# Gathering the tails of q, k and v once, starting loads by the state of the queue, and converting weights one piece ahead

## The chip, the cores and the metric

The kernel runs on one core of one Trainium2 chip. The metric is device time in microseconds (us) of one execution. An execution has five engines at work side by side: TensorE (PE, with its weight loads shown apart as PEld), VectorE (DVE), ScalarE (ACT), GpSimd (POOL) and SyncE (SP). Here SP issues nearly all DMA transfers, one after the other, and 16 DMA engines carry them out. Each engine works through its own instructions in the order in which the program was written; an instruction that waits for another engine or for a transfer holds up everything behind it on its engine.

## The reference

```
def sm_attn(qq, kk, vv):                       # 8 batches, 8 heads, sequence 576, head size 64
    s = scale * qq @ kk.T
    a = exp(s - max(s)); a = a / (sum(a) + 1e-9)
    return a @ vv
p_packed = sm_attn(p, k, v)                    # 32 packed rows a head
x = sm_attn(q, p_packed, p_packed)             # as [8, 576, 512], the 8 heads side by side
u = x + (x.T @ U @ V).T                        # U: 576x32, V: 32x576, mixing along the sequence
out = u + relu(u @ w1) @ w2                    # w1: 512x2048, w2: 2048x512
```

q, k, v and p are float32; U, V, w1 and w2 are float64 and come to the chip as pairs of 32-bit words, so that the kernel itself turns them into float32.

## The kernel before, in words

**Main work.** The last line of the reference is nearly all of the arithmetic. It runs in two sweeps over the eight batches, each with one half of the 2048 inner columns, in 8 slices of 128. For each slice `gemm1` makes relu(u w1) for 128 columns (12 matmuls 128x288 into h_ps; the packed attention is folded into the weights beforehand, so that w1 appears as wth and wtl), ACT and DVE split the result into a high part hh and a low part hl, and `gemm2` of the slice before adds 12 matmuls 128x512 into o. Each product is three matmuls (high by high, high by low, low by high; lines 166 to 170).

**Side work.** Everything else that the first sweep needs is written as chains, Python generators that yield after each step: `turn_p` (line 416) and `packs` (430) make the packed rows of a batch, once for each group g of four heads, from k and v; `load_q` (493), `attention` (500) and `mixing` (527) make u of a batch, and store it as its parts ah and al; `fold` (582) makes wth and wtl of a batch and a quarter of the columns; `convert` (273) turns pieces of w1 and w2 into float32, and `uv_chain` (319) does so for U and V.

**Who sets the order.** The class `Chains` (lines 19 to 102) is a planner that runs while the program is written. It keeps a clock of its own, times at which it thinks that ACT, DVE, POOL and the DMA queue (`free`) and the PSUM banks come free, and counts of shared buffers (`xt`, the tiles into which q, k and v are loaded; `ppT`, `wt` and so on). After each piece of gemm1 and gemm2 the kernel calls `place`, which emits up to four steps of chains that are ready by this model, the one with the earliest due time first; `until` (97) emits steps until the chains named are done, with no gemm between. The times are guesses in the source, such as `step(0, ("DMA", 4.3))` for the loads of k and v of one group; `HOP` is the guess for the way from one engine to the next. What comes out is a fixed order of instructions on each engine. At run time nothing of the planner is left: an engine meets its instructions in that order, and waits where data isn't there.

**Loads.** A tile `xt` holds 576 rows of 4 heads: the first 512 rows (the main part, 512 KB) by one DMA (`load_main`, 355), the other 64 (the tail) by four DMAs of 16 KB for k and q (`load_x`, 361) or two of 32 KB for v (`load_v`, 368). Loads of k and v of one batch and group thus are eight DMAs, those of q of a batch ten.

**Conversion.** A piece is 512 KB of float64. `load_bits` brings it into one of two buffers `bits`, by one or two DMAs. `float32_1` (223) takes the absolute value of the high words on ACT into the one tile `ts` (line 227), then works on it with two DVE operations (228, 229) into `wd`; `float32_2` (231) adds sign and low bits with two more (233, 234), and then the buffer is free and the load of the piece after next is issued. For w2 an ACT copy makes the high part w2h (301) and POOL the low part (302). A first chain converts 16 pieces in batch 0 (numbered from 0 below; pieces 0 to 3 are the first quarter of w1, 4 and 5 the first two of w2), the later ones the other halves of w2 and w1.

**The start.** Before the first gemm the kernel emits `until("attention0", "fold000", "w2_0")` (645). Batch b+1 starts its gemms when its `attention` and `fold` chains are done.

## Time and profile before

| what | value |
| --- | --- |
| median of 3 runs | 929.35 us (926.53 to 931.5) |
| profiled execution, its own time | 931.87 us |
| its span, first to last instruction | 930.0 us |
| mean granted TensorE clock | 0.934 of full speed |
| PE busy | 839.7 us, 90% of the span |
| DVE, ACT, POOL busy | 432.5, 313.2, 93.9 us |
| DMA | 73,369 packets, 105.48 MB, 113 GB/s |
| read from and written to DRAM | 70.84 MB and 33.63 MB |
| DMAs for tails in groups of four heads | 64 for k, 64 for q (16 KB each), 32 for v (32 KB each) |

A row of a timeline gives the start, the duration, the engine, the line of the kernel, the operation, the tile written and the tile read, and in brackets how long the engine had been idle and who ended that. A row of the stretches gives the stretch, its length, the busy time of each engine with the number of its instructions, the granted TensorE clock as a part of full speed (PEclk), the busy share of the DMA engines and the rate. "SPq" is the time in which SP issues a DMA.

### The profile page before, as it was taken

Reading aid. Unit: us, or ns where it says so; the run is one execution under the profiler, and the core shown is the slowest. Engines: PE = TensorE matmul, PEld = TensorE weight load, DVE = VectorE, ACT = ScalarE, POOL = GpSimd, SP = SyncE. Lnnn points to the kernel's source line nnn. Section 1 sums busy time; section 2 is a strip of 40 time slices with the busy share of each in tenths; the row PEclk is TensorE's granted clock in tenths of the full one; section 3 lists DMA queues with packets and bytes.
Section 4 is the critical chain, followed back from the end, with each engine's and each line's share of the span. In section 5 each row is a group of like instructions: output and inputs, shape, how many; then the busy total and the mean of one; then the engine's idle time right before and its main releaser. Section 6 shows DMA issues by size and latency. Waiting matters only on the chain.

```text
span 930.0 us, 15444 instructions
## 1 busy us (share of the span) xinstructions
PE 839.7 (90%) x5760; PEld 668.7 (72%) x5760; DVE 432.5 (47%) x1154; ACT 313.2 (34%) x949; POOL 93.9 (10%) x111
## 2 busy tenths in 40 slices
PE   4467488999997899999979999999999999999997
PEld 2336256766875586886667887888888888888886
DVE  1774576364576455543735742342324232432332
ACT  2542244433444434443332422232223222222220
POOL 0121123011122112110111200000000000000000
PEclk9757569998997999999979999999999999999999
DMA  8627642243368443431212242721224040404022
GB/s 209 182 75 216 163 135 83 95 124 121 118 208 256 123 118 135 130 109 48 74 77 77 97 142 74 261 71 72 68 97 143 1 152 13 142 28 137 21 71 68
DMA packets 73369, 105.48 MB, mean 113 GB/s; under 512 B 15952, under 2 KB 47056, under 8 KB 73296
## 3 DMA queue, kind: packets, MB, share of 16 engines
q1 hardware_dynamic: 72976, 103.45, 35.0%
q10 hardware_dynamic: 320, 1.05, 0.5%
q8 instruction: 46, 0.75, 0.3%
q14 instruction: 27, 0.22, 0.1%
HBM read 70.84 MB, written 33.63 MB: 112 GB/s over the span
## 4 chain that ended last, share of the span: by engine, by line
PE 80%; DMA 7%; DVE 6%; ACT 3%; issue 2%; SPq 1%; POOL 0%; ACTq 0%; DVEq 0%
PE o L168 16%; PE o L169 15%; PE o L170 15%; PE h_ps L168 7%; PE h_ps L169 7%; PE h_ps L170 7%; PE t_ps L589 4%; PE t_ps L382 3%; DMA bits<-in_moe_w_ch_dram 2%; PE t_ps L399 2%; PE t_ps L409 2%; PE t_ps L543 1%; DMA sum<-ev 1%; PE t_ps L474 1%; DMA xt<-in_v_dram 1%
## 5 line engine op out<-in xcount | busy, mean ns | idle before, releaser
L691 DVE SCALAR_TENSOR_TENSOR hl<-h_ps,hh 128x256 fp32r<-128x256 f32 x256 | 108.1, 422 | 278.1 <-ACT hjh L689 277.5
L168 PE MATMUL o<-w2h,hh 128*128 128x512 f32 x512 | 212.9, 416 | 3.3 <-DVE ev L715 2.5
L689 ACT ACTIVATE hh<-h_ps 128x256 fp32r<-128x256 f32 x256 | 98.4, 386 | 335.5 <-PE h_ps L170 335.4
L169 PE MATMUL o<-w2l,hh 128*128 128x512 f32 x512 | 203.2, 397 | 1.4 <-POOL w2l L302 1.4
L170 PE MATMUL o<-w2h,hl 128*128 128x512 f32 x512 | 202.8, 396 | 0.0
L168 PE MATMUL h_ps<-ah,wth 128*128 128x288 f32 x512 | 160.1, 313 | 2.4 <-ACT ah L562 1.9
L169 PE MATMUL h_ps<-al,wth 128*128 128x288 f32 x512 | 155.8, 304 | 0.3
L170 PE MATMUL h_ps<-ah,wtl 128*128 128x288 f32 x512 | 155.2, 303 | 0.0
L168 PEld LDWEIGHTS o<-w2h,hh 128*128 128x128 f32 x512 | 97.5, 191 | 42.0 <-issue 21.2
L168 PEld LDWEIGHTS h_ps<-ah,wth 128*128 128x128 f32 x512 | 100.4, 196 | 19.1 <-issue 12.3
L170 PEld LDWEIGHTS o<-w2h,hl 128*128 128x128 f32 x512 | 97.5, 190 | 21.4
L169 PEld LDWEIGHTS o<-w2l,hh 128*128 128x128 f32 x512 | 97.7, 191 | 14.9 <-POOL w2l L302 2.2
L169 PEld LDWEIGHTS h_ps<-al,wth 128*128 128x128 f32 x512 | 100.2, 196 | 5.0 <-POOL al L563 1.4
L170 PEld LDWEIGHTS h_ps<-ah,wtl 128*128 128x128 f32 x512 | 100.4, 196 | 0.0
L593 DVE TENSOR_TENSOR wtl<-t_ps,wth 128x512 fp32r<-128x512 f32 x64 | 41.2, 686 | 49.8 <-ACT wth L592 49.7
L592 ACT CAST wth<-t_ps 128x512 fp32r<-128x512 f32 x64 | 34.4, 589 | 51.6 <-PE t_ps L589 51.6
L383 ACT COPY xT<-t_ps 128x512 f32<-128x512 f32 x64 | 37.1, 588 | 41.4 <-PE t_ps L382 41.2
L382 PE MATMUL t_ps<-ident,xt 128*128 128x128 f32 x256 | 44.0, 307 | 7.5 <-DMA xt<-in_k_dram 4.6
L689 ACT ACTIVATE hjh<-h_ps 128x32 fp32r<-128x32 f32 x256 | 50.0, 195 | 0.0
L382 PEld LDWEIGHTS t_ps<-ident,xt 128*128 128x128 f32 x256 | 34.7, 158 | 16.2 <-DMA xt<-in_k_dram 4.7
L691 DVE SCALAR_TENSOR_TENSOR hjl<-h_ps,hjh 128x32 fp32r<-128x32 f32 x256 | 46.2, 181 | 0.0
L589 PE MATMUL t_ps<-w1t,ppT 64*32 64x512 f32 x512 | 39.1, 644 | 3.6 <-DVE xT L389 1.5
(120 smaller groups left out, 954.1 us busy)
## 6 DMA issues: line engine op xcount, KB each, us to landing
xt<-in_k_dram SPq DMA_DIRECT2D x16, 512.0 KB, 4.8
xt<-in_v_dram SPq DMA_DIRECT2D x16, 512.0 KB, 4.6
xt<-in_q_dram SPq DMA_DIRECT2D x16, 512.0 KB, 4.5
bits<-in_moe_w_ch_dram SPq DMA_DIRECT2D x16, 512.0 KB, 3.8
sum<-ev SPq DMA_DIRECT2D x32, 256.0 KB, 2.3
part<-sum SPq DMA_DIRECT2D x32, 256.0 KB, 6.2
out_dram<-ev SPq DMA_DIRECT2D x32, 256.0 KB, 2.5
bits<-in_moe_w_ch_dram SPq DMA_DIRECT2D x28, 256.0 KB, 4.7
```

The lines of the kernel that those rows point to most:

```text
L168: nc.tensor.matmul(ps, lhsT=lh, rhs=rh, start=start, stop=False)
L169: nc.tensor.matmul(ps, lhsT=lh, rhs=rl, start=False, stop=False)
L170: nc.tensor.matmul(ps, lhsT=ll, rhs=rh, start=False, stop=stop)
L382: nc.tensor.transpose(t_ps[:, P * a:P * a + P], pairs[:, P * c:P * c + P], ident)
L383: nc.scalar.copy(t[:, 2 * h2:2 * h2 + 2, HT:HS], t_ps.rearrange("p (h x) -> p h x", h=2))
L399: nc.tensor.matmul(ss[r][hs, :HS], lhsT=lT[rs, g, hs], rhs=t[rs, h, HT * (1 - r):HT * (1 - r) + HS], start=True, stop=True)
L409: nc.tensor.transpose(t_ps[:, o:o + P], src[:, BLOCK[kk]:BLOCK[kk] + P], ident)
L589: nc.tensor.matmul(f_ps[g][xs], lhsT=ppT[b][gs, g, xs], rhs=w1_slice(x, 2 * sw + c)[gs], start=True, stop=True)
L592: nc.scalar.copy(hi[:, g], f_ps[g])
L593: nc.vector.tensor_tensor(lo[:, g], f_ps[g], hi[:, g].bitcast(F32), op=ALU.subtract)
L689: nc.scalar.activation(hi, src, AF.Relu)
L691: nc.vector.scalar_tensor_tensor(lo, src, 0.0, hi.bitcast(F32), op0=ALU.max, op1=ALU.subtract)
```

## The change

Three things change.

1. A new chain `gather` copies the tails of all of k, q and v from the inputs to three tensors in DRAM, laid out as the `xt` tiles want them: one DMA for k, one for q, eight for v, 3 MB in all. It is due right after q of batch 0 is loaded. The `packs` chains wait for it in the plan. For b > 0 `load_x` and `load_v` then issue two DMAs each, the main part and one tail of 64 KB. Batch 0 loads its tails as before.
2. In the plan a chain with `load=True` (`packs`, and `load_q` for b > 0) starts only when the modelled DMA queue is through. The guessed costs of loads, and of a hop, change, and the `xt` buffers go from 7 to 6.
3. In `convert` the absolute value of piece i+1 is emitted right behind the DVE part of `float32_1` of piece i, with two `ts` tiles, and not at a step of its own; the pause with the due time now lies between `float32_1` and `float32_2`, and a piece of w1 goes on to the next without the planned wait.

All line numbers of the changed kernel are higher than those of before, by 4 at the conversion, by some 30 at the loads and behind.

```diff
--- before.py
+++ after.py
@@ -26,7 +26,8 @@
-    HOP = 0.12
+    HOP = 0.2
 
     def __init__(self, banks, **resources):
         self.now, self.left, self.done, self.flags = 0.0, {}, {}, set()
@@ -35,8 +36,8 @@
         self.resources = resources
         self.slow, self.horizon = 1.0, 0.0
 
-    def add(self, name, due, gen, after=(), need=0, take=()):
-        self.left[name] = dict(due=due, at=self.now, end=self.now, gen=gen, after=after, need=need, take=take)
+    def add(self, name, due, gen, after=(), need=0, take=(), load=False):
+        self.left[name] = dict(due=due, at=self.now, end=self.now, gen=gen, after=after, need=need, take=take, load=load)
 
     def give(self, *names):
         for n in names:
@@ -45,6 +46,7 @@
     def ready(self, name):
         c = self.left[name]
         return (c["at"] <= self.now
+                and (not c["load"] or self.free["DMA"] <= self.now)
                 and (c["due"] <= self.horizon or max(self.free["DVE"], self.free["ACT"]) <= self.now)
                 and all(n in self.flags or n in self.done and self.done[n] <= self.now for n in c["after"])
                 and all(t <= self.now for t in self.banks[:c["need"]])
@@ -65,7 +67,7 @@
         c = self.left[name]
         for r in c["take"]:
             self.resources[r] -= 1
-        used = c["need"]
+        used, c["load"] = c["need"], False
         try:
             pe, ops, c["need"], c["take"], due, wait, c["after"] = next(c["gen"])
             at = self.spend(pe, ops)
@@ -157,7 +159,7 @@
     HM = SM // 2
     HT = ST // 2
     MAIN = (slice(0, HM), slice(HS + HT, S))
-    NX = 7
+    NX = 6
 
     LEAST = 1.125 * 2.0 ** -15
 
@@ -212,7 +214,7 @@
         return pipe.tile([P, 512], I32, name="wd", bufs=2)
 
     def test_tile():
-        return pipe.tile([P, 512], F32, name="ts", bufs=1)
+        return pipe.tile([P, 512], F32, name="ts", bufs=2)
 
     def out_tile(dtype=F32):
         return pipe.tile([P, 512], dtype, name="ev", bufs=3)
@@ -220,11 +222,12 @@
     def bits_tile():
         return pipe.tile([P, 512, 2], I32, name="bits", bufs=2)
 
-    def float32_1(x, t, raw):
-
-
-        high = raw[:, :, 1]
-        nc.scalar.activation(t, high.bitcast(F32), AF.Abs)
+    def float32_0(t, raw):
+        nc.scalar.activation(t, raw[:, :, 1].bitcast(F32), AF.Abs)
+
+    def float32_1(x, t):
+
+
         nc.vector.tensor_single_scalar(t, t, LEAST, op=ALU.max)
         nc.vector.tensor_scalar(x, t.bitcast(I32), 3, 0x3FFFFFF8, op0=ALU.logical_shift_left, op1=ALU.bitwise_and)
 
@@ -234,7 +237,8 @@
         nc.vector.scalar_tensor_tensor(out.bitcast(I32), low, 29, x, op0=ALU.logical_shift_right, op1=ALU.bitwise_or)
 
     def float32_of(x, t, raw):
-        float32_1(x, t, raw)
+        float32_0(t, raw)
+        float32_1(x, t)
         float32_2(x, raw, x)
         return x.bitcast(F32)
 
@@ -280,21 +284,28 @@
                 bits[i] = load_bits(items[i][2][0], queue if i < 2 else None)
                 side.spend(0, [("DMA", 1.9)])
 
-        def words(i):
-            xi, t = word_tile(), test_tile()
-            float32_1(xi, t, bits[i])
-            return xi
+        ts = {}
+
+        def test(i):
+            if i < n:
+                ts[i] = test_tile()
+                float32_0(ts[i], bits[i])
+                side.spend(0, [("ACT", 0.67)])
 
         load(0)
         load(1)
         yield step(0, ("DMA", 0.0))
-        xi = words(0)
-        yield step(0, ("ACT", 0.67), ("DVE", 0.9))
+        test(0)
+        yield step(0, ("ACT", 0.0))
         for i, (name, due, (_, parts, after)) in enumerate(items):
             split = callable(parts)
+            xi = word_tile()
+            float32_1(xi, ts.pop(i))
+            test(i + 1)
+            yield step(0, ("DVE", 0.95), due=due, wait=False)
             float32_2(xi, bits.pop(i), xi if split else parts)
             load(i + 2)
-            yield step(0, ("DVE", 1.4))
+            yield step(0, ("DVE", 1.45), wait=split)
             if split:
                 hi, lo = parts()
                 x = xi.bitcast(F32)
@@ -304,9 +315,6 @@
                     after((hi, lo))
                 side.spend(0, [("ACT", 0.62), ("POOL", 1.3)])
             side.flags.add(name)
-            if i + 1 < n:
-                xi = words(i + 1)
-                yield step(0, ("ACT", 0.67), ("DVE", 0.9), due=items[i + 1][1])
 
     def reload_w2(kt):
         for t, x in zip(w2_tiles(kt), "hl"):
@@ -352,6 +360,21 @@
+    tails = {x: dram.tile([2 * B, P * 2 * D], F32, name=f"tail{x}", tag=f"tail{x}") for x in "kqv"}
+
+    def gather():
+        for x, src in (("k", k), ("q", q)):
+            nc.sync.dma_start(out=tails[x].rearrange("u (h x) -> (u h) x", h=4),
+                              in_=src[:, :, SM:].rearrange("b h t d -> (b h) (t d)"))
+        for r in range(2):
+            for h in range(4):
+                nc.sync.dma_start(
+                    out=tails["v"].rearrange("u (r i h d) -> r h u i d", r=2, i=32, h=4)[r, h],
+                    in_=v[:, :, SM:].rearrange("b (g h) (i r) d -> r h (b g) i d", g=2, r=2)[r, h])
+        yield step(0, ("DMA", 6.0))
+        side.flags.add("gather")
+
     def load_main(src, b, g):
         x = x_tile()
         nc.sync.dma_start(out=x[:, :4].rearrange("p h x -> p (h x)").rearrange("p (h x) -> p h x", h=4),
@@ -360,6 +383,10 @@
 
     def load_x(src, b, g):
         x = load_main(src, b, g)
+        if b > 0:
+            name = "q" if src is q else "k"
+            nc.sync.dma_start(out=x[:, 4, :2 * D], in_=tails[name][2 * b + g].rearrange("(p x) -> p x", p=P))
+            return x
         for h in range(4):
             nc.sync.dma_start(out=x[32 * h:32 * h + 32, 4, :2 * D],
                               in_=src[b, 4 * g + h, SM:].rearrange("(i r) d -> i (r d)", r=2))
@@ -367,6 +394,9 @@
 
     def load_v(b, g):
         x = load_main(v, b, g)
+        if b > 0:
+            nc.sync.dma_start(out=x[:64, 4], in_=tails["v"][2 * b + g].rearrange("(p x) -> p x", p=64))
+            return x
         for r in range(2):
             nc.sync.dma_start(out=x[32 * r:32 * r + 32, 4].rearrange("p (h d) -> p h d", h=4),
                               in_=v[b, 4 * g:4 * g + 4, SM:].rearrange("h (i r) d -> r i h d", r=2)[r])
@@ -418,7 +448,7 @@
         pn = s1.tile([P, 2, 2, D], F32, name="pn", bufs=2)
         for z in range(2):
             nc.sync.dma_start(out=pn[:, :, z], in_=p[b].rearrange("(g h) n d -> (h n) g d", g=2))
-        yield step(0, ("DMA", 0.8), need=1, take=("pT",))
+        yield step(0, ("DMA", 0.9), need=1, take=("pT",))
         t_ps = bank()
         pT[b] = s1.tile([P, 2, P], F32, name="pT", bufs=1)
         for i in range(2):
@@ -431,7 +461,7 @@
 
         kx, vx = load_x(k, b, g), load_v(b, g)
         side.flags.add(f"packs{b}{g}l")
-        yield step(0, ("DMA", 4.3), need=1, take=("xT",))
+        yield step(0, ("DMA", 1.8 if b > 0 else 3.4), need=1, take=("xT",))
         kT = s1.tile([P, 4, HS + HT], F32, name="xT", bufs=2)
         yield from turn(kx, kT, need=2, take=("e",), after=(f"pT{b}",))
         side.give("xt")
@@ -493,7 +523,7 @@
     def load_q(b):
 
         xq[b] = [load_x(q, b, g) for g in range(2)]
-        yield step(0, ("DMA", 4.2))
+        yield step(0, ("DMA", 1.8 if b > 0 else 4.2))
 
     es, aTs = {}, {}
 
@@ -605,7 +635,7 @@
         side.add(f"pT{b}", line(0, b - 2, b % 2), turn_p(b), free + (f"pT{b - 1}",), take=("ppT",))
         for g in range(2):
             side.add(f"packs{b}{g}", line(0, b - 2, (1 if b % 2 and b > 1 else 5) + g), packs(b, g),
-                     (f"packs{b - 1}{g}l",) + free, take=("xt", "xt"))
+                     (f"packs{b - 1}{g}l", "gather") + free, take=("xt", "xt"), load=True)
 
     def add_fold(sw, b, c):
         after = [f"w1_{x}_{2 * sw + c}" for x in range(4)]
@@ -616,7 +646,8 @@
         side.add(f"fold{sw}{b}{c}", line(sw, b, 4 * c) - 1, fold(sw, b, c), after, need=2, take=("wt",))
 
     def add_attention(b):
-        side.add(f"q{b}", line(0, b, 0) - 4, load_q(b), (f"mix{b - 1}",) if b else ("packs01l",), take=("xt", "xt"))
+        side.add(f"q{b}", line(0, b, 0) - 4, load_q(b), (f"mix{b - 1}",) if b else ("packs01l",), take=("xt", "xt"),
+                 load=b > 0)
         for g in range(2):
             side.add(f"scores{b}{g}", line(0, b, 0) - 3 + 0.1 * g, attention(b, g), (f"q{b}", f"packs{b}{g}"), need=1,
                      take=("xT",))
@@ -640,6 +671,7 @@
         side.left[f"scores0{g}"]["due"] = -7 + 0.1 * g
     side.left["attention0"].update(due=-6, after=("scores00", "scores01", "uv"))
     side.add("uv", -4.8, uv_chain(), after=("packs01l",))
+    side.add("gather", -4.9, gather(), after=("q0",))
     add_packs(1)
     add_fold(0, 0, 0)
     side.until("attention0", "fold000", "w2_0")
```

How the program's order moves on the engines that the prediction speaks of, rows as they stand in the two programs (line, operation, tile written and read, shape, and a count where rows repeat):

SP, from the loads of p for batch 1 on, before. `bits` are pieces for the conversion, `xt<-in_k` and `xt<-in_v` with 128x4x256 the main parts for batch 1, the smaller ones tails; vd and v_348 carry V.

```order
L420 DMA pn<-in_p_dram 128x2x64 x2
L357 DMA xt<-in_k_dram 128x4x256
L364 DMA xt<-in_k_dram 32x128 x4
L357 DMA xt<-in_v_dram 128x4x256
L371 DMA xt<-in_v_dram 32x4x64 x2
L330 DMA vd<-vx 128x144
L333 DMA v_348<-vd 32x576 x4
L357 DMA xt<-in_k_dram 128x4x256
L364 DMA xt<-in_k_dram 32x128 x4
L357 DMA xt<-in_v_dram 128x4x256
L371 DMA xt<-in_v_dram 32x4x64 x2
L270 DMA bits<-in_moe_w_ch_dram 64x1024 x2
```

SP, the same place, after the change:

```order
L450 DMA pn<-in_p_dram 128x2x64 x2
L368 DMA tailk<-in_k_dram 64x4096
L368 DMA tailq<-in_q_dram 64x4096
L372 DMA tailv<-in_v_dram 16x32x64 x8
L338 DMA vd<-vx 128x144
L341 DMA v_327<-vd 32x576 x4
L274 DMA bits<-in_moe_w_ch_dram 64x1024 x4
L274 DMA bits<-in_moe_w_ch_dram 128x1024 x2
L274 DMA bits<-in_moe_w_ch_dram 64x1024 x2
L517 DMA ppTd_83<-ppT 128x256
L380 DMA xt<-in_k_dram 128x4x256
L388 DMA xt<-tailk 128x128
```

The ten DMAs of the gather stand ahead of V and of the third piece of the conversion, where the loads of k and v for batch 1 stood; these now stand behind five loads of pieces.

ACT at the start, before. `ts<-bits` is the absolute value for one piece; eT, ppT, pT, two and xT belong to the packed rows and to the attention of batch 0.

```order
L456 COPY eT<-t_ps 128x512
L482 COPY ppT<-t_ps 128x128
L227 ACTIVATE ts<-bits 128x512
L426 ACTIVATE pT<-t_ps 128x256
L383 COPY xT<-t_ps 128x2x256 x2
L477 ACTIVATE two<-t_ps,rs 128x128
L482 COPY ppT<-t_ps 128x128
L383 COPY xT<-t_ps 128x2x256
L227 ACTIVATE ts<-bits 128x512
L383 COPY xT<-t_ps 128x2x256 x3
L514 ACTIVATE e<-e 128x576
```

ACT at the start, after the change:

```order
L226 ACTIVATE ts<-bits 128x512
L486 COPY eT<-t_ps 128x512
L456 ACTIVATE pT<-t_ps 128x256
L512 COPY ppT<-t_ps 128x128
L226 ACTIVATE ts<-bits 128x512 x5
L413 COPY xT<-t_ps 128x2x256
L507 ACTIVATE two<-t_ps,rs 128x128
L413 COPY xT<-t_ps 128x2x256
L512 COPY ppT<-t_ps 128x128
L413 COPY xT<-t_ps 128x2x256 x2
L312 CAST w2h_501<-wd 128x512
L226 ACTIVATE ts<-bits 128x512
```

Five absolute values, those of pieces 1 to 5, now stand in a row ahead of the four copies of q of batch 0 (xT), and that of piece 6 behind these; next stand four casts of V, three copies of k of batch 1 and the first exp of the attention of batch 0.

PE at the end of batch 0, after the change, from the last piece of gemm2 that is written in it (e and xt here are the packed rows and the loads of batches 1 and 2, `xT,ppT` the scores of the attention of batch 1, aT its result on the way to the mixing):

```order
L172 MATMUL o<-w2h_1247,hl 128x512
L441 MATMUL t_ps<-ident,e 64x128
L412 MATMUL t_ps<-ident,xt 128x128 x4
L504 MATMUL t_ps<-xt,eT 32x64 x20
L416 MATMUL t_ps<-ident,xt 128x128
L511 MATMUL t_ps<-ident,two 128x128
L429 MATMUL t_ps<-xT,ppT 32x288 x8
L412 MATMUL t_ps<-ident,xt 128x128 x8
L416 MATMUL t_ps<-ident,xt 128x128
L412 MATMUL t_ps<-ident,xt 128x128 x8
L416 MATMUL t_ps<-ident,xt 128x128
L429 MATMUL t_ps<-xT,pT 32x288 x8
```

PE before, around the same scores (the second group of heads of batch 1; L589 is a fold of batch 0):

```order
L481 MATMUL t_ps<-ident,two 128x128
L386 MATMUL t_ps<-ident,xt 128x128
L589 MATMUL t_ps<-w1t_162,ppT 32x512 x2
L589 MATMUL t_ps<-w1t_163,ppT 32x512 x2
L589 MATMUL t_ps<-w1t_164,ppT 32x512 x2
L589 MATMUL t_ps<-w1t_165,ppT 32x512 x2
L399 MATMUL t_ps<-xT,ppT 32x288 x8
L168 MATMUL h_ps_1263<-ah,wth 128x288
L169 MATMUL h_ps_1263<-al,wth 128x288
L170 MATMUL h_ps_1263<-ah,wtl 128x288
```

Before, gemm1 of four slices of batch 0 followed these scores; in the changed program no gemm follows them until batch 1 begins.

## The prediction

> **What bounds the kernel now.** I read the page's busy times, then the stretches, then the timelines of PE, ACT and SP in the poor stretches, and last the DMA rows.
>
> ```profile
> PE 839.7 (90%) x5760; PEld 668.7 (72%) x5760; DVE 432.5 (47%) x1154; ACT 313.2 (34%) x949; POOL 93.9 (10%) x111
> ...
> 0.00:70.00 70.00, 37.54 (x379) 23.95 (x380) 38.46 (x97) 28.83 (x70) 10.10 (x18) 0.76 0.58 155
> 70.00:90.00 20.00, 17.99 (x91) 15.37 (x90) 10.54 (x26) 6.39 (x20) 4.23 (x4) 0.81 0.70 214
> 90.00:100.00 10.00, 0.00 (x0) 0.00 (x0) 0.00 (x0) 0.47 (x1) 0.00 (x0) 0.55 0.89 228
> 100.00:130.00 30.00, 22.82 (x148) 12.66 (x149) 22.57 (x45) 11.10 (x25) 5.66 (x5) 0.56 0.38 115
> 130.00:162.00 32.00, 29.00 (x214) 21.48 (x213) 21.93 (x51) 16.55 (x46) 10.02 (x11) 0.97 0.35 111
> 162.00:275.00 113.00, 108.67 (x879) 83.78 (x879) 60.60 (x166) 49.05 (x143) 17.82 (x20) 0.97 0.41 132
> 275.00:325.00 50.00, 38.20 (x303) 28.11 (x302) 29.32 (x67) 21.20 (x56) 10.45 (x12) 0.88 0.61 191
> 450.00:500.00 50.00, 41.32 (x243) 30.11 (x243) 25.14 (x57) 15.92 (x40) 9.07 (x9) 0.83 0.12 46
> 525.00:930.00 405.00, 398.87 (x2405) 336.97 (x2404) 142.55 (x434) 101.08 (x366) 0.00 (x0) 1.00 0.27 92
> ```
>
> PE is busy 90% of the span, and from 525 on all but 6 of 405 us: the second sweep has nothing to give. What can move lies before: PE is idle for 32.5 us up to 70, for 10 from 90 to 100, for 7.2 from 100 to 130 (with the clock at 0.56), for 11.8 at 275 to 325 and for 8.7 at 450 to 500. The first gemm starts at 69.68, that of batch 1 at 161.91:
>
> ```profile
> 69.68 0.58 PE L168 MATMUL h_ps<-ah,wth 128*128 128x288 f32 x1 [1.86 <-ACT ah L562]
> ...
> 161.91 0.38 PE L168 MATMUL h_ps<-ah,wth 128*128 128x288 f32 x1
> ```
>
> The hole at 90 is one absolute value on ACT, whose piece SP issued at 92.52, behind 16 us of loads for q, k and v, most of it tails (1.89 us for four, 0.39 for a main part); everything behind it on ACT waits too:
>
> ```profile
> 99.53 0.66 ACT L227 ACTIVATE ts<-bits 128x512 f32<-128x512 f32 x1 [12.18 <-DMA bits<-in_moe_w_ch_dram]
> ```
> ```profile
> 76.26 1.06 SPq L357 DMA_DIRECT2D xt<-in_q_dram  x1
> ...
> 88.14 0.39 SPq L357 DMA_DIRECT2D xt<-in_k_dram  x1
> 88.57 1.89 SPq L364 DMA_DIRECT2D xt<-in_k_dram  x4
> ...
> 92.52 1.57 SPq L270 DMA_DIRECT2D bits<-in_moe_w_ch_dram  x3
> ```
>
> **The change, part by part: the gather.** On SP it stands where the loads of batch 1 stood, ahead of V (vd, then four copies of it) and of piece 2:
>
> ```profile
> 23.03 0.95 SPq L420 DMA_DIRECT2D pn<-in_p_dram  x2
> ...
> 28.36 0.35 SPq L330 DMA_DIRECT2D vd<-vx  x1
> 31.78 1.71 SPq L333 DMA_DIRECT2D v<-vd  x4
> ...
> 37.65 1.18 SPq L270 DMA_DIRECT2D bits<-in_moe_w_ch_dram  x2
> ```
>
> No DRAM-to-DRAM copy of this kind is in the trace, so I bound it. A stretch of small packets and one of large ones give a price for a packet:
>
> ```profile
> DMA packets 3341, 2.58 MB, mean 215 GB/s; under 512 B 730, under 2 KB 3341, under 8 KB 3341
> ...
> q1 hardware_dynamic: 3341, 2.58, 72.0%
> ```
> ```profile
> q1 hardware_dynamic: 3888, 7.73, 52.5%
> ```
>
> The first is 12 to 24 us, the second 560 to 600. 72.0% of 12 us on 16 engines is 41 ns for a packet of 772 bytes, 52.5% of 40 us is 86 ns for one of 1,988: 13 ns and 37 ns a KB. The gather of v has runs of 256 bytes, 4,096 of them: at 22 ns on 16 engines 5.7 us. Its bounds are 3.5 (1.05 MB at the first stretch's 299 GB/s of busy time) and 10.6 (as dear as packets of 772 bytes). k and q, 2.1 MB in long runs, take 5.7 us at the second stretch's 368 GB/s, at most 7.0 at 299. So the gather takes 11.4 us (9.2 to 17.6). It starts near 26, when the loads ahead of it are in, and ends at 37.5. V's round trip behind it took 3.1 us alone (28.71 to 31.78); since vd may move along with the last packets I take 2. Then come 1.7 for V's copies and 1.2 to issue piece 2, and from there to its absolute value 5.0 as before (38.83 to 43.87, below): T2 = 47.4 instead of 43.87, with bounds of 45 and 54. By a rule of the Trainium skill (DMA: Bandwidth & Descriptors, Specifications) a transfer under 512 bytes is a read-modify-write, which I estimate at twice the work: v would take 11.4, T2 would be 53.1, and my sum 942 instead of 936.4. No row shows a copy that settles it.
>
> **The absolute values ahead.** Before, they were spread among the copies; the third waited 1.35 us and no more:
>
> ```profile
> 33.20 0.68 ACT L227 ACTIVATE ts<-bits 128x512 f32<-128x512 f32 x1
> 33.78 1.54 ACT L383 COPY xT<-t_ps 128x512 f32<-128x512 f32 x3
> ...
> 43.87 0.66 ACT L227 ACTIVATE ts<-bits 128x512 f32<-128x512 f32 x1 [1.35 <-DMA bits<-in_moe_w_ch_dram]
> ...
> 51.93 0.68 ACT L514 ACTIVATE e<-e 128x576 f32<-128x576 f32 x1
> ```
> ```profile
> 31.10 0.70 DVE L233 SCALAR_TENSOR_TENSOR wd<-bits,wd 128x512 int32<-128x512 int32 x1
> 31.83 0.69 DVE L234 SCALAR_TENSOR_TENSOR w1t<-bits,wd 128x512 int32<-128x512 int32 x1
> ```
> ```profile
> xt<-in_k_dram SPq DMA_DIRECT2D x16, 512.0 KB, 4.8
> ...
> bits<-in_moe_w_ch_dram SPq DMA_DIRECT2D x16, 512.0 KB, 3.8
> ```
>
> Now those of pieces 1 to 5 stand in one row on ACT, and two `bits` buffers mean that piece 4 is loaded only when piece 2 has been through DVE. From T2: 0.7 for the absolute value, 0.9 and 1.4 on DVE, 0.2 of hops, 0.5 of issue and 3.8 of landing bring piece 4 at T2+7.5, piece 5 two us later; the row ends at T2+9.9. Only then do the copies of q for attention 0 begin, which ran at 29.79 to 35.3 before. Piece 6 comes by the same round trip at T2+14.6, and ahead of attention 0's first exp stand also V's casts (1.5) and three copies of k of batch 1, whose load is issued behind piece 6 and lands 4.8 later: T2+19. The packed rows' exps and the second exp of attention 0 follow at T2+23. From there to the first gemm it took 17.8 us before (51.93 to 69.68); the operations alone add up to 13, and since fewer pieces lie between now, I take 15. First gemm: T2+38 = 85.4, 15.7 later than before. No work hides this: no gemm can run ahead of it.
>
> **Batch 0.** The pieces now stand on SP ahead of q, k and v of later batches, so the hole at 90 goes. What is late next is attention 1: its second scores stand behind the last gemm written in batch 0, where four slices covered the rest of it before. A batch with its side work took 56.5 us (113 for batches 1 and 2), and I take that for batch 0 too: the ACT waits below eat what its lighter side work saves. The chain from those scores to batch 1 is scores 1, two DVE transposes 1.7, maximum and subtraction 2, exp 0.7 and the 17.8 above, 23 in all, and with the packed rows' operations between them 25, PE idle. Batch 1 starts at 85.4+56.5+25 = 166.9: **5.0 later** than before. The price of the tail is 0 if gemms did cover it.
>
> **Later batches.** Each later piece's absolute value is emitted about 1.5 us of plan behind its own load, so ACT waits for most of a landing, 2 to 4 us. The relu copies stand behind it; they are covered by one slice of gemm2, 2.86 us here:
>
> ```profile
> 132.32 0.50 PE L168 MATMUL o<-w2h,hh 128*128 128x512 f32 x1
> ...
> 135.18 0.29 PE L168 MATMUL h_ps<-ah,wth 128*128 128x288 f32 x1
> ```
>
> So a piece costs 0 to 1.2, and 16 pieces 0 to 19; I take 0.6 each, 10. Against it the stalls of 20.5 us at 275 to 325 and 450 to 500 may shrink, by better spaced loads and truer prices in the plan; bounds are 0 and 20.5, and I take 8. **Together +2** (-12 to +12). SP issues 14 DMAs fewer a batch, 6.6 us at 0.47; its turn was on the path in the hole, counted above, and I count the rest at nothing beyond those bounds. The seventh `xt` buffer I count at nothing as well: q, one group's k and v, and a mixing take two each, six.
>
> **The sum.** 931.87 + 5.0 + 2 = 938.9 for an execution like the profiled one, which lay 2.5 above the median: **936.4**.
>
> **The rivals.** *B, faster: the hole goes and little comes back.* The gather ends early (T2 = 45), attention 0 goes at its bare length (first gemm at T2+33 = 78), batch 0 at 50 with a warm clock, since 22.8 us of PE work ran at 0.56 behind the hole, and the tail at 22.5: batch 1 at 150.5, 11.4 earlier, and later batches gain 2: 918.5, or 916 on the median. For it speaks that DMA share 0.89 beside PE idle is just what the change takes away; against it the five absolute values in a row. A rule of the Trainium skill (DMA: Bandwidth & Descriptors, Rules for kernel authors) is on its side: transfers under 64 KB are mostly overhead and are to be merged. *C, no change: the two cancel.* T2 = 45, the first gemm at 83, a tail of 20: batch 1 at 159.5, 2.4 earlier, later +2: 931.5, or 929. Here the queue was never what counted but in one place, and the change does not do what it is built for. *D, much slower:* the small runs of v's gather cost 10.6 and those of k and q 7.0, T2 = 54, the first gemm at T2+41 = 95, batch 1 at 176.5, and ACT's waits show in full later (+10): 956.5, or 954 on the median. It decides from T2 = 52 on. For it speaks that 730 of the 3,341 packets of the dear stretch were under 512 bytes; against it that the queue has nothing else to carry then.
>
> **How the numbers follow.** The chance of my forecast (A, 930 to 946 by its own terms) is 0.39, of B 0.31, of C 0.19, of D 0.11. A measurement of this kernel can tell about 0.5%, 4.6 us, from no change. A and D are slower: 0.50; C is the same: 0.19; B is faster: 0.31. The range, from B's end to D's, is 914 to 955.
>
> **What would show it.** Right: ACT has one long wait for `bits` at 35 to 60 with copies of q behind it, the first gemm is at 80 to 95, no PE hole at 90 to 100 of the old kind, and PE idles some 25 us just ahead of batch 1, which starts at 160 to 175. Wrong: the first gemm before 78 (then the gather or the row of absolute values is cheap), batch 1 before 157, or batches 3 to 6 shorter by over 10 us together, in which case the later stalls were due to the loads.

## The result

The changed kernel takes **961.37 us** (median of 4 runs, 960.29 to 961.91) where the kernel before takes 929.42: **1.0345** times as long, 95% interval 1.0315 to 1.0374. The direction was the forecast one, the size was not: 936.4 was predicted, with 955 as the far end.

The stretches of the profile after, cut at the first gemm, the last gemm written in batch 0, the first gemm of batch 1, and the start of the second sweep (start, length, busy time of PE, PEld, DVE, ACT and POOL, clock, DMA share, rate):

```profile
0.00:86.00 86.00, 37.23 (x379) 24.02 (x380) 38.14 (x97) 29.99 (x71) 10.73 (x20) 0.70 0.61 168
86.00:146.00 60.00, 46.17 (x261) 35.15 (x261) 40.81 (x89) 22.14 (x63) 10.68 (x8) 0.89 0.58 175
146.00:180.00 34.00, 23.28 (x206) 13.62 (x207) 14.38 (x37) 11.95 (x28) 7.04 (x9) 0.66 0.30 92
180.00:602.00 422.00, 383.43 (x2788) 296.78 (x2788) 217.17 (x562) 162.05 (x468) 63.97 (x74) 0.93 0.35 113
602.00:960.00 358.00, 353.18 (x2131) 299.74 (x2129) 120.56 (x372) 87.11 (x321) 0.00 (x0) 1.00 0.27 92
```

The same stretches of the kernel before:

```profile
0.00:70.00 70.00, 37.54 (x379) 23.95 (x380) 38.46 (x97) 28.83 (x70) 10.10 (x18) 0.76 0.58 155
70.00:162.00 92.00, 69.81 (x451) 49.51 (x451) 55.04 (x122) 34.51 (x91) 19.91 (x20) 0.76 0.49 147
162.00:572.00 410.00, 379.07 (x2804) 295.19 (x2804) 218.39 (x564) 162.66 (x469) 63.86 (x75) 0.95 0.37 117
572.00:930.00 358.00, 353.32 (x2131) 300.02 (x2130) 120.59 (x372) 87.19 (x321) 0.00 (x0) 1.00 0.27 92
```

PE does nearly the same work everywhere (37 us ahead of the first gemm in both), in longer stretches. By the first gemm of each stretch in the timelines, the 30.1 us of the span are 16.2 up to the first gemm (69.68 to 85.83), 1.6 in batch 0 (92.2 to 93.9), and 12.1 from batch 1 to the second sweep (409.7 to 421.8). The second sweep is the same within 0.2 us.

In all three stretches one instruction waits longer than before: the absolute value of a piece on ACT. The view of its line, whole run, first before, then after (sum of ACT's idle time ahead of it, and how often):

```profile
  DMA bits<-in_moe_w_ch_dram: 13.7, 3
```
```profile
  DMA bits<-in_moe_w_ch_dram: 82.7, 21
```

ACT now stands still 21 times for a piece that is on its way, 82.7 us in all. The timeline of ACT after shows where: the row of five at the start, then one or two in each slice of batch 0, with the relu copies (L721) behind them.

```profile
31.20 0.70 ACT L226 ACTIVATE ts<-bits 128x512 f32<-128x512 f32 x1
45.98 0.66 ACT L226 ACTIVATE ts<-bits 128x512 f32<-128x512 f32 x1 [14.08 <-DMA bits<-in_moe_w_ch_dram]
48.20 0.67 ACT L226 ACTIVATE ts<-bits 128x512 f32<-128x512 f32 x1 [1.56 <-DMA bits<-in_moe_w_ch_dram]
52.65 0.66 ACT L226 ACTIVATE ts<-bits 128x512 f32<-128x512 f32 x1 [3.78 <-DMA bits<-in_moe_w_ch_dram]
55.38 0.66 ACT L226 ACTIVATE ts<-bits 128x512 f32<-128x512 f32 x1 [2.08 <-DMA bits<-in_moe_w_ch_dram]
55.95 0.56 ACT L413 COPY xT<-t_ps 128x512 f32<-128x512 f32 x1
...
92.25 0.66 ACT L226 ACTIVATE ts<-bits 128x512 f32<-128x512 f32 x1 [3.59 <-DMA bits<-in_moe_w_ch_dram]
95.44 0.66 ACT L226 ACTIVATE ts<-bits 128x512 f32<-128x512 f32 x1 [2.53 <-DMA bits<-in_moe_w_ch_dram]
96.00 0.37 ACT L721 ACTIVATE hh<-h_ps 128x256 fp32r<-128x256 f32 x1
...
102.81 0.66 ACT L226 ACTIVATE ts<-bits 128x512 f32<-128x512 f32 x1 [6.35 <-DMA bits<-in_moe_w_ch_dram]
...
114.30 0.67 ACT L226 ACTIVATE ts<-bits 128x512 f32<-128x512 f32 x1 [6.35 <-DMA bits<-in_moe_w_ch_dram]
```

Late in the first sweep the last conversion has a row of four (`x2` merges the first two), and there the third one holds ACT for 9 us:

```profile
538.00 1.23 ACT L226 ACTIVATE ts<-bits 128x512 f32<-128x512 f32 x2
548.20 0.66 ACT L226 ACTIVATE ts<-bits 128x512 f32<-128x512 f32 x1 [8.97 <-DMA bits<-in_moe_w_ch_dram]
550.90 0.66 ACT L226 ACTIVATE ts<-bits 128x512 f32<-128x512 f32 x1 [2.04 <-DMA bits<-in_moe_w_ch_dram]
551.46 0.37 ACT L721 ACTIVATE hh<-h_ps 128x256 fp32r<-128x256 f32 x1
```

PE, in the same two places, waits for the h_ps banks that these relu copies and the DVE part behind them empty; the other two rows are the first gemm and the first of batch 1:

```profile
85.83 0.61 PE L170 MATMUL h_ps<-ah,wth 128*128 128x288 f32 x1 [2.45 <-DVE wtl L623]
...
97.15 0.58 PE L170 MATMUL h_ps<-ah,wth 128*128 128x288 f32 x1 [7.25 <-DVE hjl L723]
...
179.69 0.61 PE L170 MATMUL h_ps<-ah,wth 128*128 128x288 f32 x1
...
554.52 0.58 PE L170 MATMUL h_ps<-ah,wth 128*128 128x288 f32 x1 [10.72 <-DVE hjl L723]
```

PE's row names DVE as the releaser; what was late is the load, two engines further back. The hole that PE had at 90 to 100 before is gone, but at 97.15 another of 7.25 us stands in its place.

### The profile page after: what moved, and what is told of

It reads as the page before. It is cut to its first block, busy times and chain, and to the rows that moved or that the text cites. A ratio compares the mean times of both kernels' runs of the same rounds, so it can differ in the third digit from the quotient of the medians.

```text
span 960.1 us, 15329 instructions
## 1 busy us (share of the span) xinstructions
PE 843.3 (88%) x5760; PEld 669.3 (70%) x5760; DVE 431.1 (45%) x1154; ACT 313.2 (33%) x949; POOL 92.4 (10%) x111
## 4 chain that ended last, share of the span: by engine, by line
PE 74%; DVE 5%; DMA 2%; ACT 2%; issue 1%; SPq 0%; ACTq 0%; DVEq 0%
PE o L170 14%; PE o L172 14%; PE o L171 14%; PE h_ps L170 7%; PE h_ps L172 7%; PE h_ps L171 7%; PE t_ps L619 4%; PE t_ps L412 2%; DMA bits<-in_moe_w_ch_dram 2%; PE t_ps L429 2%; PE t_ps L439 1%; PE t_ps L504 1%; PE t_ps L573 1%; DVE ts L231 1%; DVE wd L236 1%
## 5 line engine op out<-in xcount | busy, mean ns | idle before, releaser
L721 ACT ACTIVATE hh<-h_ps 128x256 fp32r<-128x256 f32 x256 | 98.3, 386 | 328.7 <-PE h_ps L172 328.0
L412 PE MATMUL t_ps<-ident,xt 128*128 128x128 f32 x256 | 46.2, 318 | 12.1 <-DMA xt<-in_k_dram 7.0
L619 PE MATMUL t_ps<-w1t,ppT 64*32 64x512 f32 x512 | 43.8, 642 | 8.2 <-DVE xT L419 3.6
L721 ACT ACTIVATE hjh<-h_ps 128x32 fp32r<-128x32 f32 x256 | 49.6, 194 | 0.0
L226 ACT ACTIVATE ts<-bits 128x512 f32<-128x512 f32 x32 | 21.4, 670 | 82.8 <-DMA bits<-in_moe_w_ch_dram 82.7
```

The costliest lines, as they stand in the source:

```text
L226: nc.scalar.activation(t, raw[:, :, 1].bitcast(F32), AF.Abs)
L412: nc.tensor.transpose(t_ps[:, P * a:P * a + P], pairs[:, P * c:P * c + P], ident)
L619: nc.tensor.matmul(f_ps[g][xs], lhsT=ppT[b][gs, g, xs], rhs=w1_slice(x, 2 * sw + c)[gs], start=True, stop=True)
L721: nc.scalar.activation(hi, src, AF.Relu)
```

## The experiments

My theory after the result: the third part of the change, the absolute value one piece ahead, costs nearly all, because ACT meets it before its data is there. The rival: the gather, whose 3 MB stand ahead of V and of piece 2 on the queue, and the loads that now start late.

The table gives the first gemm, the first of batch 1 and the start of the second sweep in the profiled execution of each kernel (first matmul into h_ps), ACT's idle time for pieces from 20 to 200 us, and the median, with the ratio to runs of the kernel before on the same chip.

| kernel | first gemm | batch 1 | second sweep | ACT for pieces | median us | ratio (95%) |
| --- | --- | --- | --- | --- | --- | --- |
| before | 69.7 | 161.9 | 571.6 | 13.5 | 929.42 | |
| after | 85.8 | 179.7 | 601.5 | 49.2 | 961.37 | 1.0345 (1.0315 to 1.0374) |
| e1 old conversion | 80.6 | 168.2 | 563.3 | 0.6 | 922.42 | 0.9942 (0.9907 to 0.9976) |
| e2 conversion alone | 76.3 | 177.0 | 592.1 | 47.7 | 952.63 | 1.0270 (1.0214 to 1.0326) |
| e3 starts by the queue alone | 70.9 | 162.9 | 569.0 | 1.3 | 927.79 | 1.0007 (0.9971 to 1.0042) |
| e4 gather alone | 79.6 | 175.9 | 582.3 | 12.0 | 942.31 | 1.0152 (1.0093 to 1.0212) |
| e5 planned wait back | 80.1 | 174.0 | 579.2 | 40.6 | 940.23 | 1.0130 (1.0096 to 1.0165) |
| e6 ahead once landed | 82.6 | 177.8 | 573.5 | 16.6 | 934.32 | 1.0065 (1.0040 to 1.0090) |
| e7 gather later | 72.3 | 170.9 | 566.5 | 7.9 | 925.23 | 0.9970 (0.9946 to 0.9995) |
| e8 attention 1 early | 85.3 | 175.6 | 597.9 | 46.9 | 960.37 | 1.0373 (1.0322 to 1.0425) |
| e9 wait back, later w1 | 88.4 | 180.1 | 583.6 | 49.7 | 944.68 | 1.0203 (1.0153 to 1.0253) |
| e10 HOP alone | 73.2 | 176.0 | 578.6 | 18.4 | 937.17 | 1.0122 (1.0074 to 1.0170) |
| e11 seven buffers | 78.6 | 162.4 | 554.6 | 0.0 | 920.99 | 0.9931 (0.9898 to 0.9964) |
| e12 gather later, seven buffers | 76.9 | 172.6 | 566.8 | 19.7 | 927.78 | 0.9999 (0.9979 to 1.0019) |

### e1: the change with the old conversion

Against the change:

```diff
-        return pipe.tile([P, 512], F32, name="ts", bufs=2)
+        return pipe.tile([P, 512], F32, name="ts", bufs=1)
...
-            xi = word_tile()
-            float32_1(xi, ts.pop(i))
-            test(i + 1)
-            yield step(0, ("DVE", 0.95), due=due, wait=False)
...
+            if i + 1 < n:
+                xi = words(i + 1)
+                yield step(0, ("ACT", 0.67), ("DVE", 0.9), due=items[i + 1][1])
```

> The change with its third part undone: gather, two loads a unit and the starts by the queue stay, the absolute values go back to where they stood before (one ts tile). Theory (the absolute values in a row hold ACT, first ahead of attention 0, then through batch 0, and leave attention 1 without cover): the first gemm comes at 72 to 80, four slices of gemm again cover attention 1 (so the program's order has it), batch 1 starts at 155 to 166, and the whole takes 922 to 937 us, 25 to 39 under the change. Rival (the gather and its place on the queue cost the time): the first gemm stays past 82, and the whole at 945 or more.

Measured: 922.42, inside the theory's range and 39 under the change; ACT waits 0.6 us for pieces instead of 49.2. Two places missed: the first gemm at 80.6 and batch 1 at 168.2 are later than expected, as the gather's share of the start stays. In the profiled executions e1 is 5.3 us ahead of the change at the first gemm, gains 6.2 more in batch 0, and 26.8 from batch 1 to the second sweep. Against the kernel before it starts 10.9 later, and takes 4.5 less in batch 0 and 14.6 less from batch 1 on. With the third part undone the change is 0.6% faster than the kernel before, which is less than what e10 below shows an order alone to be worth.

### e2: the conversion alone

The kernel before with the conversion of the change (`float32_0`, `test`, two `ts` tiles, no planned wait for pieces of w1), and:

```diff
-    NX = 7
+    NX = 6
```

> The kernel before with the third part alone (and 6 xt buffers instead of 7, since the second ts tile has no room otherwise); no gather, no starts by the queue. Theory: most of the loss is there without the gather: batch 1 past 172, the whole at 943 to 962 us. Rival (the gather): the whole within 5 us of 929.

Measured: 952.63, batch 1 at 177.0. Without gather and without starts by the queue, 25 to 27 of the 32 us are there (2.7% by the ratio, 26.9 us by the medians on that chip). PE shows what it shows in the whole change; its first gemm, and its two longest idle times behind that, the second at the row of four:

```profile
76.33 0.61 PE L168 MATMUL h_ps<-ah,wth 128*128 128x288 f32 x1 [2.44 <-DVE wtl L599]
...
117.47 0.69 PE L388 MATMUL t_ps<-ident,xt 128*128 128x128 f32 x2 [8.11 <-DVE wtl L599]
...
544.98 0.58 PE L168 MATMUL h_ps<-ah,wth 128*128 128x288 f32 x1 [8.90 <-DVE hjl L697]
```

### e3 and e4: the second and the first part alone

e3, against the kernel before:

```diff
-    HOP = 0.12
+    HOP = 0.2
+                and (not c["load"] or self.free["DMA"] <= self.now)
-    NX = 7
+    NX = 6
...
+                 load=b > 0)
```

e4, against the kernel before, with `gather`, its three tensors, and `load_x` and `load_v` of the change:

```diff
+    side.add("gather", -4.9, gather(), after=("q0",))
```

> The kernel before with the second part alone: loads start by the state of the modelled queue, the hop costs 0.2 in the plan, 6 xt buffers; the old prices of loads, no gather, old conversion. Theory: the hole at 90 to 100 shrinks as pieces come ahead of loads; 918 to 932 us. Rival (starting loads late starves the packed rows): 935 or more, with waits of PE for xt of k above those before (4.6 us in all).

> The kernel before with the first part alone: gather and two loads a unit, at the old prices in the plan, no start by the queue, old conversion, 7 xt buffers. Theory: the gather puts off V and piece 2 by 2 to 6 us at the start, and shorter load runs on SP give most of it back at 90 to 100; 922 to 936 us. Rival (the gather is the cost): 940 or more, first gemm past 80.

Measured: e3 927.79, no difference. The hole at 90 to 100 is gone there (ACT waits 1.3 us for pieces, and PE is busy 5.64 of these 10 us instead of 0.00), and batch 1 still starts at 162.9: **taking the hole away did not by itself bring the end of batch 0 forward**. PE idles 21.8 us in batch 0 there and 22.2 before; the idle time has moved to smaller waits.

e4 942.31, where my theory said 922 to 936: the rival's range for the whole, with the first gemm at 79.6 just short of the rival's 80. The first gemm moves by 9.9 us (10.9 in e1). Of the 9.9, only 3.5 are there at the absolute value of piece 2, which comes at 47.41 instead of 43.87; the other 6.4 come behind it, where ACT waits for piece 3, whose load SP issues at 49.27, behind the loads of k and v for batch 1, and at 39.57 before:

```profile
47.41 0.66 ACT L227 ACTIVATE ts<-bits 128x512 f32<-128x512 f32 x1 [1.86 <-DMA bits<-in_moe_w_ch_dram]
...
58.07 0.66 ACT L227 ACTIVATE ts<-bits 128x512 f32<-128x512 f32 x1 [6.64 <-DMA bits<-in_moe_w_ch_dram]
```

So part of the 9.9 is the order, and whether the rest of the 1.5% is the gather's, e10 below puts in doubt.

### e5, e6 and e9: what of the conversion costs

All three against the change; first e5:

```diff
-            yield step(0, ("DVE", 1.45), wait=split)
+            yield step(0, ("DVE", 1.45))
```

e6, where the added step ends in the plan when the queue is through and a landing is over:

```diff
-            test(i + 1)
             yield step(0, ("DVE", 0.95), due=due, wait=False)
+            if i + 1 < n:
+                yield step(0, ("DMA", 0.0))
+            test(i + 1)
```

e9, with `back=True` for the conversions of the third and fourth quarter of w1 alone:

```diff
+    def convert(items, queue=None, back=False):
-            yield step(0, ("DVE", 1.45), wait=split)
+            yield step(0, ("DVE", 1.45), wait=split or back)
```

> The change with one word undone: a piece of w1 again waits in the plan for its DVE work before it goes on to the next; the absolute value stays one piece ahead. In the program's order the row of five on ACT is gone (the absolute values stand one by one among the copies), but attention 1's second scores still stand behind the last gemm of batch 0. Theory (two costs: the row at the start, and the uncovered attention 1): first gemm at 79 to 84, the tail ahead of batch 1 still 25 to 36, batch 1 at 170 to 178, in all 940 to 957 us. Rival (all the loss is the row of waits): 922 to 935 us.

> The change, with the absolute value of the next piece still ahead, but in the plan only once its load has landed (a step that waits for the modelled queue and a landing). Two slices of gemm then cover attention 1 instead of none. Theory (what is lost is ACT waiting for pieces that are still on their way): ACT's waits for pieces up to 200 us fall from 53 to under 25 us, and the whole is at 922 to 938 us. Rival (the second tile and the order ahead as such are bad, by the DVE and ACT time they take early): 945 us or more.

> The change, with the planned wait of a piece of w1 put back in the two last conversions alone (third and fourth quarter of w1). The program is the same up to batch 5; the row of four absolute values near its end is gone. Theory (that row is the idle 10.7 us of PE at 554 and more before it): batch 1 at 179.7 as in the change, batches 5 and 6 together 8 to 18 us shorter (130.0 before this), the whole at 943 to 953 us. Rival (those batches lose it to something else, such as stores and part sums on the queue): 957 or more.

Measured: 940.23, 934.32 and 944.68, each in the theory's range. e9 is the cleanest: the program is the change's up to the first part of batch 5, batch 1 starts at 180.1, and batches 5 and 6 take 110.9 us instead of 130.0, a little more than expected (8.1 us less in batch 5, 11.0 in batch 6). It undoes the change in two places. One is the row of four, in batch 6. The other is a single absolute value in batch 5, which in the change holds ACT and then PE too:

```profile
452.69 0.66 ACT L226 ACTIVATE ts<-bits 128x512 f32<-128x512 f32 x1 [6.47 <-DMA bits<-in_moe_w_ch_dram]
```
```profile
454.41 0.58 PE L170 MATMUL h_ps<-ah,wth 128*128 128x288 f32 x1 [3.53 <-DVE hjl L723]
```

Leaving out one planned wait in the two last conversions thus costs 16.7 of the 32 us by the medians, and 13 by the ratios (1.0345 and 1.0203), as e9 was timed on another chip. e5 takes that wait back everywhere: the first gemm comes 5.7 sooner, the later batches 16.6 sooner, batch 0 takes the same 93.9. In e6 the ACT waits fall to 16.6 as foreseen, and the later batches gain 26 us on the change, but batch 0 still takes 95.2: there, waits for pieces are not the whole story.

### e8: attention 1 brought forward

```diff
-        side.add(f"q{b}", line(0, b, 0) - 4, load_q(b), ...
+        side.add(f"q{b}", line(0, b, 0) - (9 if b == 1 else 4), load_q(b), ...
-            side.add(f"scores{b}{g}", line(0, b, 0) - 3 + 0.1 * g, attention(b, g), ...
+            side.add(f"scores{b}{g}", line(0, b, 0) - (8 if b == 1 else 3) + 0.1 * g, attention(b, g), ...
```

> The change, with earlier due times for the loads of q and the scores of batch 1 alone (by 5 slices in the plan). The row of five and the other rows of absolute values stay, but in the program's order four slices of gemm of batch 0 again follow attention 1's second scores. Theory (the uncovered attention 1 costs what PE idles there, 34.6 us from the last gemm to batch 1, less what stays uncovered before the change too): batch 1 at 160 to 170 instead of 179.7, the whole at 941 to 953 us. Rival (attention 1 is bound by ACT's waits for pieces, so the same time is lost ahead of the gemms instead of behind them): batch 1 at 175 or later, the whole at 955 or more.

Measured: 960.37, the rival's range. Four slices of gemm do stand behind attention 1's scores again, yet the slice that began at 120.8 in the change begins at 134.2 here, and batch 1 at 175.62. The idle time moved from behind the gemms to ahead of them:

```profile
70.00:85.00 15.00, 11.58 (x147) 7.84 (x147) 10.00 (x25) 8.27 (x22) 5.49 (x8) 0.72 0.07 27
85.00:150.00 65.00, 45.39 (x259) 35.06 (x259) 47.18 (x99) 23.75 (x62) 14.54 (x12) 0.76 0.57 173
150.00:185.00 35.00, 30.08 (x253) 22.59 (x253) 11.95 (x34) 14.62 (x42) 3.54 (x6) 0.85 0.28 93
```

The stretch from the last gemm of batch 0 to batch 1 is 18.4 us here instead of 34.7, and the gemms end 12.2 later. So the uncovered tail was, for the most part, where batch 0's loss showed and not what caused it.

### e10: what a re-roll of the plan is worth

```diff
-    HOP = 0.12
+    HOP = 0.13
```

> The kernel before with one guess of the plan changed by a hundredth, HOP 0.13 instead of 0.12, which moves single steps all over the order and nothing else. It measures what the plan's luck is worth, against which the other differences stand. Theory (orders that differ in single steps are worth a few us): 922 to 938 us. Rival (the plan is fragile, and any re-roll can bring 15 us or more): outside 915 to 945.

Measured: 937.17, 1.2% slower than the kernel before, just inside the theory's range. It does the same work with the same loads, and batch 1 starts 14 us later. The old hole is there, on ACT and then on PE:

```profile
98.86 0.66 ACT L227 ACTIVATE ts<-bits 128x512 f32<-128x512 f32 x1 [11.15 <-DMA bits<-in_moe_w_ch_dram]
99.42 0.57 ACT L383 COPY xT<-t_ps 128x512 f32<-128x512 f32 x1
99.89 0.39 ACT L689 ACTIVATE hh<-h_ps 128x256 fp32r<-128x256 f32 x1
```
```profile
100.77 0.96 PE L399 MATMUL t_ps<-xT,ppT 64*32 64x288 f32 x7 [10.17 <-ACT hjh L689]
```

It is not what makes the difference, as PE's hole was longer in the kernel before:

```profile
100.72 0.48 PE L386 MATMUL t_ps<-ident,xt 128*128 128x128 f32 x1 [12.20 <-ACT xT L383]
```

Of the 14 us, 3.5 are there at the first gemm; in batch 0 PE then idles 29.8 us instead of 22.2, and its operations take 3.0 longer. Which steps of the order do this is not shown.

A difference of 1% between two of these kernels can therefore be the order alone. Each timing is sharp; what it is a timing of is one order out of many. That holds for e4's 1.5%, of which only the start has a direct reading, and for the gains of e1 and e11. It is far below e1 against the change (39 us) and under half of e2's 2.7%; but it is a single change of a guess, and how far others would move the time was not tried. In e9 the order up to batch 5 is the change's own.

### e7, e11 and e12: a version that beats both

e7, against e1, and with `b > 1` for `b > 0` where tails are loaded; e11 is e1 with seven `xt` buffers, e12 is e7 with seven:

```diff
-    side.add("gather", -4.9, gather(), after=("q0",))
+    side.add("gather", 2.0, gather(), after=("q1",))
```

> The change with the old conversion, and the gather put off: it is emitted in batch 0, behind the loads of q for batch 1; batches 0 and 1 load their tails themselves, the others from the gathered ones. Theory (the gather's 10 to 12 us of queue ahead of V and piece 2 put the first gemm off by 10, and nothing else about it costs): first gemm at 69 to 73 instead of 80.6, batch 1 at 157 to 163, in all 910 to 920 us. Rival (those 10 us are lost again in batch 0, where the queue is the bound with or without it): 920 to 928 us.

> The change with the old conversion, and with the seven xt buffers of before instead of six. Theory (with gather and starts by the queue the seventh buffer is not needed): within 5 us of the 922.4 that the same kernel took with six. Rival (the seventh buffer lets a load start earlier where PE waits for xt): 917 or less.

> The change with the old conversion, the gather put off into batch 0 (batches 0 and 1 load their own tails), and seven xt buffers. Theory (the late gather starts the gemms 8 us sooner, the seventh buffer gave batch 0 back its cover): first gemm at 70 to 74, batch 1 at 155 to 163, the whole 908 to 917 us. Rival (what the early start wins is lost in batch 0 whatever the buffers, and differences of this size are the plan's luck): 917 to 930 us.

Measured: 925.23, 920.99 and 927.78. The late gather does bring the first gemm to 72.3, and batch 1 comes at 170.94 all the same, 2.7 later than in e1:

```profile
72.31 0.40 PE L170 MATMUL h_ps<-ah,wth 128*128 128x288 f32 x1 [1.85 <-DVE wtl L617]
...
170.94 0.61 PE L170 MATMUL h_ps<-ah,wth 128*128 128x288 f32 x1
```

The rival held in e7 and e12: what the start wins, batch 0 loses. In e12 the first gemm (76.9, with 70 to 74 expected) and batch 1 (172.6, with 155 to 163 expected) missed as well. e11 is the fastest kernel found, 0.7% under the kernel before with an interval of 0.4 to 1.0%; that is about the size that a measurement can tell, and less than a re-roll is worth. In none of the kernels does batch 1 start before 161.9, with or without the hole, with the first gemm anywhere from 70 to 81 in those with the old conversion. What holds batch 0 at 84 to 103 us in these is left open.

## Why the prediction was wrong, step by step

- **The start was right.** T2, the absolute value of piece 2, was put at 47.4 and came at 45.98; the row of five ended at T2+10.1 (predicted 9.9); the first gemm was put at 85.4 and came at 85.83. Both steps are found again in the runs with one part each: the gather alone puts T2 3.5 later (e4; 3.5 forecast), and with the conversion alone it takes 37.4 from T2 to the first gemm (e2; 38 forecast, 25.8 before). At the first gemm itself the two runs are 9.9 and 6.6 later than the kernel before. That these nearly add up to the 16.2 of the change is luck: e4 loses another 6.4 behind T2, waiting for piece 3, and in e2 T2 comes 4.9 sooner than before.
- **The gather's price was right.** The DMA view of the change, 26 to 40 us:

```profile
DMA packets 4759, 3.28 MB, mean 234 GB/s; under 512 B 4503, under 2 KB 4631, under 8 KB 4631
...
q1 hardware_dynamic: 4759, 3.28, 83.7%
```

  83.7% of 14 us on 16 engines are 187.5 us; 13 ns a packet and 37 ns a KB make 183. The Trainium skill (DMA: Bandwidth & Descriptors, Specifications) has transfers under 512 bytes as read-modify-writes; the twofold price that I had estimated from it does not show here.
- **Batch 0 failed: "the hole at 90 goes", -10.7 was forecast and +1.6 measured.** Two terms of it were off. I took 56.5 us up to the last gemm (half of the stretch from 162 to 275; from first gemm to first gemm, batches 1 and 2 took 57.9 and 65.8), reasoning that ACT waits would only eat what the lighter side work saved: they added up to 27.7 us between 85 and 146 (the rows of ACT's timeline), against one of 12.2 before, and the gemms took 59.2 (85.83 to about 145). And the tail was 34.7 instead of 25, at a clock of 0.66 (146 to 180), with no gemm between the steps of the chain. The forecast had PE idle there; it was at side work for 23.28 of the 34 us from 146 to 180. Behind both is a reading of the profile before that the runs do not bear out: I took a hole of 10 us with no PE work in it as 10 us to be had. e3 takes the hole away and gains nothing; e1 and e11, with the gather as well, take 87.7 and 83.8 in batch 0 instead of 92.2. So something besides the hole held batch 0's end, and what it was stays open; the conversion, with its waits, took 6.2 us there (e1 against the change).
- **The later batches failed: +2 forecast, +12.1 measured.** The 2 were 10 for ACT's waits less 8 for stalls that shrink, and both terms were too small, the first by more: e1 takes 14.6 less there than the kernel before, and the change 26.8 more than e1, though their orders differ in other steps too. A piece was priced at 0.6 us, for waits of 2 to 4 us against a cover of 2.86. Already a piece by itself could cost more: at 452.69 ACT waits 6.47 and PE idles 3.53. And in the row of four the third waits for a load that can be issued only when an earlier piece is through DVE, with the relu copies behind it: 8.97 on ACT, 10.72 on PE. About 2.7 of the 8.97 come from a slow DVE operation (last section). With both places undone (e9), batches 5 and 6 take 19.1 less. I had followed such a row at the start, and did not look for another, though ACT's order showed it. All later batches together then take 403.5 (e9), 6.2 less than before: the gaining side of the bounds that I had set.
- **Rival D** came near in size (954), half for a wrong reason: it took a dear gather, with T2 at 54, and T2 came at 45.98. Its other reason, ACT's waits in full in the later batches at +10, is what was measured.
- **What would have helped:** counting rows of absolute values in ACT's order over the whole program, and taking no gain from the hole without asking what else ended at 161.9.

## What to carry to other kernels

An operation placed "one ahead" on an engine that works in order is ahead only if its data has landed by then; otherwise each of its waits becomes a wait of everything behind it, and in a row of several, where a load can start only when an earlier piece has left its buffer, the wait for a whole round trip comes on top (here up to 8.97 us). Look for such rows in the order of the whole program, and do not read a hole in the busiest engine as time to be had before you know what else ends at the same place. Where a planner fixes the order from guesses, time a change of one guess by a hundredth first: here that alone moved the time by 1.2%, and differences below it say nothing by themselves on the idea that was tried.

## What was not expected of the hardware

A copy from DRAM to DRAM in runs of 256 bytes costs no more for a packet than the line through loads of 772 and 1,988 bytes gives (187.5 against 183 us of engine time for 4,759 packets). SP's row for the eight copies of v lasts 10.10 us, where I had counted 0.47 for an issue. Taken one by one, six of the eight issues take 0.60 to 0.73 us, and the third and the fifth 2.81 and 3.05; whether these two wait for earlier transfers is not shown.

```profile
26.48 10.10 SPq L372 DMA_DIRECT2D tailv<-in_v_dram  x8
36.70 0.54 SPq L338 DMA_DIRECT2D vd<-vx  x1
39.47 1.72 SPq L341 DMA_DIRECT2D v<-vd  x4
```
```profile
27.86 2.81 SPq L372 DMA_DIRECT2D tailv<-in_v_dram  x1
```
```profile
31.49 3.05 SPq L372 DMA_DIRECT2D tailv<-in_v_dram  x1
```

In the row of four, the first DVE operation takes 3.10 us, where the median of this operation is 0.43, and so the load behind it is issued later. It stands beside memsets of POOL and ends shortly after them:

```profile
538.70 3.10 DVE L231 TENSOR_SCALAR ts<-ts 128x512 f32<-128x512 f32 x1
```
```profile
538.57 0.99 POOL L836 MEMSET rdh<- 128x512 f32 x2
...
540.95 0.57 POOL L836 MEMSET ajl<- 128x256 f32 x2
```

The kernel before and e8 have one such operation each, of 3.08 and 3.09 us, also beside these memsets. That the memsets cause it is not shown, as no run moves them alone.
